# A two-layer decode kernel: filler matmuls in the chain's gaps, the second layer's scores in two halves, a centred x copied out by ScalarE, and the seven-row final FFN placed later

## The chip, the cores and the metric

The kernel runs on one core of a Trainium2 chip. The metric is the device time of one execution in microseconds. A profile records one execution: its span, when each engine was busy, what released each wait, and the clock that TensorE was granted.

## The reference, cut to what matters

Eight sequences (B = 8) each decode one token through two layers that share their weights and caches. A layer is attention over the last 1024 positions of a cache and then an FFN, both with a residual.

```python
x = x + A(layernorm(x))     # wq, softmax over 1024 keys, 16 query heads on 8 kv heads of 256, wo
x = x + B(layernorm(x))     # w1 (448 -> 1792), silu, w2 (1792 -> 448)
x = x + A(layernorm(x))     # the same weights, the same K and V
x = x + B(layernorm(x))

# A, with W = 1024, Dh = 256, D = 448
q = (x @ wq).reshape(B, 1, 16, 256).transpose(0, 2, 1, 3)
k, v = (jnp.repeat(c[:, :, Sk - W:, :], 2, axis=1) for c in (k_cache, v_cache))
p = softmax(einsum("bhqd,bhkd->bhqk", q, k) * 256 ** -0.5)
o = einsum("bhqk,bhkd->bhqd", p, v);  return o.transpose(0, 2, 1, 3).reshape(B, 1, 4096) @ wo
```

A sequence's K and V (8 + 8 tiles of 512 KB) are read once and used by both layers.

## The kernel before, in words

**Loads.** All K and V tiles pass through a ring of R = 30 slots in SBUF. SyncE issues one DMA per tile (K at L467, V at L472) in the order K of sequence b, V of b, K of b+1 and so on. A load waits until the tile that used its slot 30 loads earlier has been read for the last time. K tiles are freed by the second layer's scores of their sequence, V tiles by its second weighted sum. So the 16 loads that follow a sequence's second scores are: the last two V of b+1, the first six K of b+2, and, once its second weighted sum is done too, the last two K and the first six V of b+2.

**One sequence.** VectorE transposes the K tiles in place in blocks (`layer1_early`, L901, 16 instructions). `scores` (L608) multiplies the query blocks `qbd` with K into a PSUM bank: four column tiles of TensorE at once, 8 steps, 32 matmuls of 512 columns for a layer. `softmax` takes the maxima (L613), spreads them by two small transposes, exponentiates on ScalarE (L629), turns the rows into columns by matmuls (L636) and copies them out. `pv_rows` (L658) and `pv_cols` (L685) make the weighted sum of V, `wo_part` (L722) the output projection. For layer 1 the row is then folded onto x (`fold`: ScalarE copies the row at L735, six matmuls of one column at L508 and L511 turn it into columns of bank YB). x sits there as raw columns and, in a sixth column, minus its mean; `xcols` (L696, VectorE) adds the mean, masks the padding and writes the bf16 columns `xbt`.

**The chain.** `feed` and `chain` carry a single token through the first FFN and the query of the second layer, step after step on different engines: `xcols`, `stats` (the variance, off to one side through ScalarE and GpSimd), w1 (L743), copy (L748), turn (`hturn`, L750), tanh (L753), hT (L756, VectorE), w2 (L759), `fold`, `xcols`, wq (L777, 32 matmuls of 512 columns), copy (L783), `q_blocks` (turn at L593, VectorE copy qT2 at L596, selection matmuls at L572, one VectorE product at L598 that writes all of `qbd`), then the second layer's scores, softmax, and weighted sum. While one sequence is in its chain, the next one's layer-1 scores are ready to run, and they are interleaved with the second layer's scores of the first.

**The end.** The second FFN is done for seven sequences at once in `final_rows` (wo of seven rows at L811, w1 at L502, w2 at L835, and so on), whose tasks lie in program order ahead of the last sequence's chain, and for the last sequence alone in `final_last`. Only these two and the last chain have a pair of filler matmuls (`keep`, L729, zero weights, 480 columns).

**Order.** All instructions are tasks of a planner (`Plan`). It knows what each task reads and writes, simulates five in-order queues with the durations in the code, and writes a fixed order for every engine; the most urgent ready task goes first, where urgency is the longest way to the end plus a table of corrections (`BIAS`). On the chip each engine runs its list in that order and waits on semaphores.

Of the kernel before, what the change touches and what calls it, by code (L numbers as in the profile page):

```python
# [4 lines left out]
BF16 = mybir.dt.bfloat16  # L5
# [14 lines left out]
       "dve:max": 0.62, "dve:qbd": 0.62, "act:maskr": 0.13, "act:var4": 0.16, "act:x2b": 0.16, "act:rsum": 0.66,  # L20
# [5 lines left out]
BIAS = {"dve.KT.a": -113.5, "pe.wo.a@7": -369.9, "pe.qsel.b": 390.4, "pe.S0.a": 152.8, "pe.l.c@8": -243.0,  # L26
        "pe.PV0.2.a@7": -51.4, "pe.l.c@7": -192.9, "pe.w18.c": -747.4, "pe.PV1.2.c": 382.0, "dve.hT.b@0": -156.7,
        "dve.qT2.b": -486.8, "dve.oTev.c@1": -161.9, "pe.wq.b": -161.9, "pe.stat.b": 114.3, "pe.stat.b@7": -142.4,
        "pe.PV0.c6.a": 734.8, "pe.PV0.c7.a@0": 159.8, "pe.xres.e": -183.3, "pe.PV1.0.c": -112.1,
        "pe.xinit8.e": -155.3, "pe.fold.a@7": -45.5, "pe.hturn.b": -26.0, "pe.stat.e": 12.5}  # L30
# [237 lines left out]
def bass_interleave_layers__sliding_block_cached__dense_activation_silu__decode_kernel(  # L268
# [9 lines left out]
    P = 128  # L278
# [24 lines left out]
    qbd = [sb(f"qbd{i}", [P, 4, 8, 16], BF16) for i in range(2)]  # L303
# [8 lines left out]
    xb0 = sb("xb0", [P, XC + 1, NB], BF16)  # L312
    f_sb = sb("f_sb", [P, 24], F32)
    b_sb = sb("b_sb", [P, 56], BF16)
# [7 lines left out]
    x2b = xb0  # L322
# [3 lines left out]
    fold8, hT = b_sb[:, 4:12], b_sb[:, 12:28]  # L326
    xl0, nm = b_sb[:, 28:36], b_sb[:, 36:37]
    xz = b_sb[:, 38:53].rearrange("p (c n) -> p c n", n=3)
# [6 lines left out]
    xh = slots[R - 2][:, 512:512 + 2 * XC * NB].rearrange("p (c n) -> p c n", n=2 * NB)  # L335
# [9 lines left out]
    C_Q, C_QT, C_ST, C_HT = 0, 128, 160, 192  # L345
    TW = ((0, 4), (4, 3), (7, 4), (11, 3))
# [46 lines left out]
    dve(lambda e: e.memset(b_sb[:, 38:53], 0.0), [], ["xbt"], 0.08, -98)  # L393
# [90 lines left out]
    def xcol(i, hi):  # L484
        return i if i < 3 else 3 + hi
# [10 lines left out]
    def proj(bank_i, col, outs, lhs, half, rhs, n):  # L496

        fns = []
        for o in outs:
            for i in range(KC):  # L500
                r = rhs(xcol(i, o // half))
                fns.append(lambda e, o=o, i=i, r=r: e.matmul(  # L502
                    bank[bank_i][:, col + (o - outs[0]) * n:col + (o - outs[0] + 1) * n], lhs(o, i), r,
                    start=(i == 0), stop=(i == KC - 1)))
        return fns

    def to_cols(bank_i, col, row, rhs, nb, prio, reads, name, shape):
        fns = [lambda e, c=c: e.matmul(bank[bank_i][xpart(c), col + c * nb:col + (c + 1) * nb], xpiece(row, c), rhs,  # L508
                                       start=False, stop=True, tile_position=xpos(c), skip_group_check=True)
               for c in range(XC)]  # L510
        fns.append(lambda e: e.matmul(bank[bank_i][:, col + XC * nb:col + (XC + 1) * nb],  # L511
                                      row[:, D:D1].broadcast_to([P, P]), rhs, start=False, stop=True,
                                      skip_group_check=True))
        pe(fns, reads, bk(bank_i), shape, prio, name)
# [24 lines left out]

    def start_rows(prio):  # L540
# [4 lines left out]
            for c in range(XC)], ["xrow", "ident"] + L, bk(YB), (NB, 1), prio)  # L545
        m58 = mask5[:].unsqueeze(2).broadcast_to([P, XC, NB])
        dve(lambda e: e.tensor_tensor(xb0[:, 0:XC, :], xp[:, 0:XC * NB].rearrange("p (c b) -> p c b", b=NB), m58,
                                      ALU.mult), bk(YB) + M5, ["xb0"], 0.2, prio)
        stats8(xb0[:, 0:XC, :], sq8, sqh8, vn8, rhalf8, LB, C_ST, NB, ["xb0"] + L, "st", prio, True)
        xcf = big8[:, 0:XC * NB].rearrange("p (c b) -> p c b", b=NB)  # L550
        dve(lambda e: e.tensor_tensor(xcf, xb0[:, 0:XC, :], nmean8.unsqueeze(1).broadcast_to([P, XC, NB]), ALU.add),
            ["xb0", "nmean8"] + L, ["big8"], 0.2, prio)
        dve(lambda e: e.tensor_tensor(xcf, xcf, m58, ALU.mult), ["big8"] + M5 + L, ["big8"], 0.2, prio)
        dve(lambda e: e.tensor_copy(xh[:, :, 0:NB], xcf), ["big8"] + L, ["xh0"], 0.15, prio)
        dve(lambda e: e.tensor_tensor(xh[:, :, NB:], xcf, xh[:, :, 0:NB], ALU.subtract), ["big8", "xh0"] + L, ["xh1"],
            0.2, prio)
        dve(lambda e: e.tensor_copy(xb0[:, XC, :], nmean8), ["nmean8"] + L, ["xm0"], 0.12, prio)
        dve(lambda e: e.tensor_tensor(xl0[:], nmean8, xb0[:, XC, :], ALU.subtract), ["nmean8", "xm0"] + L, ["xl0"], 0.15,
            prio)
        pe(proj(YB, 0, range(NCH), wq_l, 16, lambda i: xh[:, i, :], 2 * NB),  # L560
           ["xh0", "xh1"] + WQ_R + L, bk(YB), (2 * NB, 1), prio, "q1")
# [8 lines left out]
    def q_sel(src, keys, prio):  # L570
        qs = bank[LB][:, C_Q:C_Q + 128].rearrange("p (t a s n) -> p s t a n", t=4, a=2, s=4)
# [4 lines left out]
    def q_view(v):  # L576
        return v.rearrange("p (n r) -> p n r", r=2).unsqueeze(2).broadcast_to([P, 64, 4, 2])

    def q_wide(m):
        return m.unsqueeze(1).unsqueeze(3).broadcast_to([P, 64, 4, 2])  # L580

    qbd_v = [t[:].rearrange("p t c (j q r) -> p (t c j) q r", q=4, r=2) for t in qbd]

    def q_blocks1(b, prio):
        qs = q_sel(q1T[:, b, :].rearrange("p (t n a) -> p t a n", t=4, n=4), [("q1r", b)], prio)
        act(lambda e: e.activation(q1s[:], qs, ACTF.Copy), bk(LB), [("pT", 0)], 0.3, prio, "q1s")  # L586
        add("pool", lambda e: e.tensor_tensor(qbd_v[0], q_view(q1s), q_wide(mask), ALU.mult),  # L587
            reads=[("pT", 0)] + MASK_R, writes=[("qbd", 0)], dur=1.1, prio=prio, name="qbd1")
# [150 lines left out]
    def feed(prio, warm):  # L739
# [14 lines left out]
        if warm:  # L754
            keep(2, prio, XB)
# [222 lines left out]
```

## Time and profile before

| what | value |
|---|---|
| time, three runs | 280.54 us median (278.52 to 284.11) |
| the profiled execution's own time | 282.43 us |
| its span | 280.6 us |
| mean TensorE clock granted | 0.812 |
| TensorE busy | 194.1 us (69%), 2963 matmuls |
| VectorE busy | 152.6 us (54%), of it 82.2 us in the 128 K transposes |
| ScalarE, GpSimd busy | 75.5 us, 21.7 us |
| read from HBM | 77.67 MB, 277 GB/s over the span |

Read it as a pipeline over sequences: a start until the first V tiles are there (48.8 us), then one period for each sequence, then an end in which nothing is loaded any more. The start of the layer-1 maximum (L613) of a sequence marks a period: for sequences 1 to 7 it lies at 72.99, 97.27, 123.68, 151.67, 178.07, 205.18 and 232.89 us. The granted clock is either 1.0 or 0.5 of full speed; the mean of 0.812 mixes the two.

### The profile page before, as it was taken

The numbers are of one execution on the slowest core, as the hardware profiler recorded it, in microseconds if no ns is written. First come the engines' busy times: TensorE is split into PE (matmuls) and PEld (weight loads), VectorE is DVE, ScalarE is ACT, GpSimd is POOL, SyncE is SP. The second block draws the span as 40 slices with busy tenths as digits, with TensorE's granted clock in tenths as the row PEclk, the third lists the DMA queues.
The fourth block names the chain that finished last, engine by engine and source line by source line (L and its number), as shares of the span: only waits on it lengthen the run. The fifth ranks groups of instructions, "written<-read, shape, count | busy, mean of one in ns | idle before, by whom it ended". The sixth has DMA issues, their size and how long they took to land.

```text
span 280.6 us, 6834 instructions
## 1 busy us (share of the span) xinstructions
PE 194.1 (69%) x2963; PEld 84.4 (30%) x2963; DVE 152.6 (54%) x392; ACT 75.5 (27%) x198; POOL 21.7 (8%) x34
## 2 busy tenths in 40 slices
PE   1050400867896887798679868996898588977575
PEld 0050100322442343234223422343234223453231
DVE  6389559249629647733864395538544844122111
ACT  2000729122223133213321331223122313223122
POOL 1200000010011002000200020010001000020000
PEclk9999955755999899669857995797589658999895
DMA  6999999999599979949992999299929993000000
GB/s 254 348 406 357 341 363 388 369 407 387 181 397 370 372 258 409 392 164 310 409 390 92 353 402 386 96 398 403 357 97 369 404 340 120 36 2 3 0 2 0
DMA packets 33757, 78.11 MB, mean 278 GB/s; under 512 B 2224, under 2 KB 8256, under 8 KB 33344
## 3 DMA queue, kind: packets, MB, share of 16 engines
q1 hardware_dynamic: 33728, 77.68, 74.9%
q8 instruction: 23, 0.38, 0.5%
q14 instruction: 6, 0.05, 0.0%
HBM read 77.67 MB, written 0.01 MB: 277 GB/s over the span
## 4 chain that ended last, share of the span: by engine, by line
PE 47%; SPq 15%; DMA 14%; DVE 12%; ACT 8%; issue 3%; POOL 1%; ACTq 0%; DVEq 0%; POOLq 0%
PE bank L608 12%; DMA slot<-in_A_k_cache_dram 10%; PE bank L777 8%; DVE slot L901 8%; PE bank L658 7%; SPq L472 6%; SPq L431 5%; PE bank L722 4%; DMA slot<-in_A_v_cache_dram 4%; PE bank L759 3%; SPq L467 3%; ACT qrow L735 2%; PE bank L685 2%; ACT qrow L783 2%; ACT e_sb L629 2%
## 5 line engine op out<-in xcount | busy, mean ns | idle before, releaser
L901 DVE STREAM_TRANSPOSE slot<-slot 128x512 uint32<-128x512 uint32 x128 | 82.2, 687 | 9.9 <-DMA slot<-in_A_k_cache_dram 9.5
L608 PE MATMUL bank<-slot,qbd 128*16 128x512 bf16 x512 | 43.3, 492 | 8.2 <-DVE slot L901 7.4
L658 PE MATMUL bank<-slot,pT_sb 128*4 128x512 bf16 x448 | 35.8, 408 | 13.9 <-DMA slot<-in_A_v_cache_dram 13.0
L777 PE MATMUL bank<-wq_sb,b_sb 128*2 128x512 bf16 x256 | 27.7, 583 | 0.0
L629 ACT ACTIVATE e_sb<-bank,mseg 128x256 bf16<-128x256 f32 x32 | 13.4, 470 | 46.0 <-DVE mseg L626 25.2
L613 DVE TENSOR_REDUCE mseg<-bank 128x2 f32<-128x512 f32 x16 | 11.1, 691 | 21.9 <-PE bank L608 21.9
L608 PEld LDWEIGHTS bank<-slot,qbd 128*16 128x16 bf16 x512 | 14.0, 102 | 27.8 <-issue 12.8
L587 POOL TENSOR_TENSOR qbd<-pT_sb,f_sb 128x512 bf16<-128x512 bf16 x8 | 8.3, 1041 | 146.2 <-ACT pT_sb L586 146.2
L658 PEld LDWEIGHTS bank<-slot,pT_sb 128*4 128x4 bf16 x448 | 11.1, 87 | 27.5 <-issue 17.9
L759 PE MATMUL bank<-w_sb,b_sb 128*1 128x449 bf16 x126 | 12.0, 473 | 6.5 <-DVE b_sb L756 6.5
L722 PE MATMUL bank<-wo_sb,oT 128*1 128x449 bf16 x256 | 16.2, 360 | 0.0
L707 POOL TENSOR_TENSOR f_sb<-f_sb 128x1 f32<-128x1 f32 x17 | 9.4, 550 | 75.2 <-ACT f_sb L705 75.1
L636 PE MATMUL bank<-ident,e_sb 128*64 128x16 bf16 x256 | 6.8, 179 | 8.2 <-ACT e_sb L629 8.1
L670 DVE TENSOR_TENSOR oT<-bank,rl_sb 128x24 bf16<-128x24 f32 x8 | 1.5, 183 | 20.0 <-PE bank L666 20.0
L586 ACT ACTIVATE pT_sb<-bank 128x128 bf16<-128x128 f32 x8 | 2.2, 278 | 35.1 <-PE bank L685 20.2
L448 DVE TENSOR_REDUCE slot<-wo_sb 128x5 f32<-128x2240 bf16 x4 | 9.7, 2479 | 3.3 <-DMA wo_sb<-in_A_wo_dram 3.3
L508 PE MATMUL bank<-b_sb,qrow 128*128 128x1 bf16 (+1 forms) x85 | 6.2, 181 | 7.6 <-ACT qrow L735 7.6
L689 DVE TENSOR_TENSOR oT<-bank,rl_sb 128x4 bf16<-128x4 f32 x16 | 2.6, 162 | 14.4 <-PE bank L685 14.4
L743 PE MATMUL bank<-w_sb,b_sb 128*1 128x512 bf16 (+1 forms) x144 | 10.1, 375 | 0.3 <-DVE b_sb L696 0.3
L696 DVE SCALAR_TENSOR_TENSOR b_sb<-bank,f_sb 128x5 bf16<-128x5 f32 x17 | 3.8, 224 | 10.9 <-PE bank L511 7.7
L508 PEld LDWEIGHTS bank<-b_sb,qrow 128*128 128x128 bf16 (+1 forms) x85 | 4.5, 106 | 17.2 <-ACT qrow L735 16.9
L783 ACT ACTIVATE qrow<-bank 128x512 bf16<-128x512 f32 x8 | 4.8, 597 | 18.1 <-PE bank L777 18.1
(151 smaller groups left out, 219.1 us busy)
## 6 DMA issues: line engine op xcount, KB each, us to landing
slot<-in_A_k_cache_dram SPq DMA_DIRECT2D x64, 512.0 KB, 9.1
slot<-in_A_v_cache_dram SPq DMA_DIRECT2D x64, 512.0 KB, 9.8
wo_sb<-in_A_wo_dram SPq DMA_DIRECT2D x1, 3584.0 KB, 31.0
wq_sb<-in_A_wq_dram SPq DMA_DIRECT2D x3, 1024.0 KB, 6.9
w_sb<-in_B_w_dram SPq DMA_DIRECT2D x1, 1568.0 KB, 21.2
w_sb<-in_B_w_dram SPq DMA_DIRECT2D x1, 1344.0 KB, 14.2
wq_sb<-in_A_wq_dram SPq DMA_DIRECT2D x2, 256.0 KB, 10.2
w_sb<-in_B_w_dram SPq DMA_DIRECT2D x2, 112.0 KB, 12.8
```

The costliest lines, as they stand in the source:

```text
L431: dma(lambda e: e.dma_start(wo_sb[:].rearrange("p (c n) -> p c n", n=DP)[:, :, 0:D], A_wo.rearrange("(c p) n -> p c n", p=P)), ["wo"], HD ...
L472: dma(lambda e: e.dma_start(slots[s].rearrange("p (q n) -> p q n", q=2), A_v_cache[b, kvh, S0:SK, :].rearrange("(q p uh) d -> p q (uh d)", ...
L508: fns = [lambda e, c=c: e.matmul(bank[bank_i][xpart(c), col + c * nb:col + (c + 1) * nb], xpiece(row, c), rhs, start=False, stop=True, til ...
L608: fns.append(lambda e, c=c, t=t, kv=kv: e.matmul(bank[sc][32 * t:32 * t + 16, :], qbd[layer][:, t, c, :], kv[:, c // 2, c % 2], start=(c = ...
L613: dve(lambda e: e.tensor_reduce(mseg[layer][:, 0:2], bank[sc][:].rearrange("p (k n) -> p k n", k=2), AX.X, ALU.max, negate=True), bk(sc), ...
L629: act(lambda e, k=k: e.activation(e_sb[:, k, :].rearrange("p (uh i ul) -> p uh i ul", uh=4, ul=2), bank[sc][:, k * 256:(k + 1) * 256].rear ...
L658: fns.append(lambda e, c=c, t=t, vv=vv: e.matmul(bank[ob][32 * t:32 * t + 4, :], pT_sb[ei][:, c, t, :], vv[:, c % 2, c // 2], start=(c == ...
L722: fns.append(lambda e, i=i, c=c, kvh=kvh: e.matmul(bank[wb][32 * c:32 * c + 1, 0:D1], oT[:, i % 2, i // 2:i // 2 + 1], wo_sb[:, i * DP:i * ...
L759: pe([lambda e, n=n, t=t, m=m: e.matmul(bank[XB][32 * (n % 4):32 * (n % 4) + 1, 0:D1], hT[:, 4 * m + t:4 * m + t + 1], w2_sb[:, (TW[t][0] ...
L777: pe([lambda e, j=j, c=c, k2=k2: e.matmul(bank[XB][32 * j:32 * j + 2, :], xz[:, xcol(c, k2), 1 - k2:3 - k2], wq_sb[:, c * HD + ((4 * k2 + ...
L783: act(lambda e: e.activation(qrow[:], bank[XB][:], ACTF.Copy), bk(XB), ["rowb"], 0.6, prio, "qrow")
L901: dve(lambda e, v=v: e.transpose(v, v), [("slot", s)], [("slot", s)], 0.67, prio, "KT")
```

## The change

- **Fillers.** `keep` goes; `fill(n)` issues n matmuls of 512 columns with zero weights into bank WB. `feed` has two after w1, three after the turn, two after w2, and `chain` two after wq, for every sequence. A key "row" keeps the chain's matmuls and the fillers in program order among themselves.
- **Scores.** The heads of a column tile are now kvh t and t+4 instead of 2t and 2t+1. Layer 2 computes its scores in two halves of 256 columns (K tiles 0 to 3, then 4 to 7), 64 matmuls instead of 32; layer 1 keeps 32 of 512. `qbd` of layer 2 is written by two VectorE products of half the size, and each half of the steps waits for its own. V is loaded in the order 0, 4, 1, 5, 2, 6, 3, 7. The product that scales the weighted sum (`oTev`) is two instructions instead of one.
- **Centred x.** Bank YB holds x minus its mean, and the mean in column 0. `fold` has eight matmuls instead of six (two more add the mean into the half columns); `xcols` is a plain copy by ScalarE. The copy of minus the mean in `final_last` goes, and qT2 moves from VectorE to ScalarE.
- **Final FFN.** `final_rows` stands behind the last chain and the last scores in program order, and its first matmul waits for the last sequence's second maximum (key "last"). Its VectorE steps for centring become one ScalarE copy.
- **Table.** `BIAS` has other entries, so the planner's order differs in places.

```diff
-    def keep(n, prio, kb):
-        pe([lambda e: e.matmul(bank[kb][:, 16:496], zero_b.broadcast_to([P, P]), wq_sb[:, 0:480],
+    def fill(n, prio):
+        pe([lambda e: e.matmul(bank[WB][:], zero_b.broadcast_to([P, P]), wq_sb[:, 0:512],
                                start=False, stop=True, skip_group_check=True) for _ in range(n)],
-           [("wq", 0), "zero_b"], bk(kb), (480, 1), prio, "keep")
+           [("wq", 0), "zero_b"], bk(WB) + ["row"], (512, 1), prio, "fill")
+    FILL = (2, 3, 2, 2)
...
     # feed: w1
-               ["xbt"] + W1_R, bk(XB), (448, 4), prio, "w1")
+               ["xbt"] + W1_R, bk(XB) + ["row"], (448, 4), prio, "w1")
         act(lambda e: e.activation(qrow[:], bank[XB][:], ACTF.Copy), bk(XB), ["rowb"], 0.6, prio, "w1row")
+        fill(FILL[0], prio)
...
         act(lambda e: e.activation(th, ht, ACTF.Tanh, scale=rhalf), bk(LB) + ["rhalf"], OT1, 0.31, prio, "tanh")
-        if warm:
-            keep(2, prio, XB)
+        fill(FILL[1], prio)
...
     # feed: behind w2
+        fill(FILL[2], prio)
...
     # chain: behind wq
         act(lambda e: e.activation(qrow[:], bank[XB][:], ACTF.Copy), bk(XB), ["rowb"], 0.6, prio, "qrow")
+        fill(FILL[3], prio)
         q_blocks(prio)
...
     def xcols(prio):
-        dve(lambda e: e.scalar_tensor_tensor(out=xbt, in0=bank[YB][:, 0:XC], scalar=bank[YB][:, XC:XC + 1],
-                                             in1=mask5[:], op0=ALU.add, op1=ALU.mult), bk(YB) + M5, ["xbt"], 0.23, prio,
-            "xb")
+        act(lambda e: e.activation(xbt, bank[YB][:, 0:XC + 1], ACTF.Copy), bk(YB), ["xbt"], 0.25, prio, "xb")
...
     def q_blocks(prio):
-        dve(lambda e: e.tensor_copy(qT2, bank[LB][:, C_QT:C_QT + 32]), bk(LB), OT1, 0.18, prio, "qT2")
+        act(lambda e: e.activation(qT2, bank[LB][:, C_QT:C_QT + 32], ACTF.Copy), bk(LB), OT1, 0.25, prio, "qT2")
...
-        dve(lambda e: e.tensor_tensor(qbd_v[1], q_view(qs), q_wide(maskr), ALU.mult), bk(LB) + ["maskr"], [("qbd", 1)], 0.7, prio,
-            "qbd")
+        for a in range(2):
+            dve(lambda e, a=a: e.tensor_tensor(qbd_v[1][:, 32 * a:32 * a + 32], *q_wide(qs[:, 64 * a:64 * a + 64], maskr),
+                                               ALU.mult), bk(LB) + ["maskr"], [("qbd", 1, a)], 0.4, prio, "qbd")
...
     def scores(b, layer, prio):
         sc = SC[layer]
-        for c in range(8):
+        for ks in ((slice(0, 2),) if layer == 0 else (slice(0, 1), slice(1, 2))):
+            for c in range(8):
...
+                    kv = kslots[:, s + 4 * ks.start:s + 4 * ks.stop - 3:4, c // 2, c % 2]
+                    fns.append(lambda e, c=c, t=t, kv=kv, ks=ks: e.matmul(
+                        bank[sc][32 * t:32 * t + 16, 256 * ks.start:256 * ks.stop], qbd[layer][:, c, t, :], kv,
+                        start=(c == 0), stop=(c == 7), tile_position=(0, 32 * t)))
...
     # to_cols, used by fold
+        fns += [lambda e, c=c: e.matmul(
+            bank[bank_i][xpart(c), col + (c + 1) * nb:col + (c + 2) * nb], m.broadcast_to([P, 64]), rhs,
+            start=False, stop=True, tile_position=xpos(c), skip_group_check=True) for c in (3, 4)]
...
     for b in range(NB):
         if b < NB - 1:
             layer1_early(b + 1)
-        else:
+        chain(b, 100 * b + 60)
+        if b == NB - 1:
+            scores(b, 1, 100 * b + 60.5)
             orow7 = final_rows(NB - 1, 100 * b + 90)
-        chain(b, 100 * b + 60)
         layer2(b)
```

## The prediction, made before the changed kernel was run

> **What bounds the kernel now.** I read first the page's slices, then a table of windows, then TensorE's timeline for one sequence, then SyncE's waits. In the slices, TensorE is busy almost throughout and its clock swings between 9 and 5; the DMA engines have a hole in each period from the sixth on.
>
> ```profile
> PE   1050400867896887798679868996898588977575
> PEclk9999955755999899669857995797589658999895
> DMA  6999999999599979949992999299929993000000
> ```
>
> The windows below are 3.41 us wide, because the openings of the clock that I found in half-microsecond windows (52.4, 69.5, 93.2, 124.1, 151.4, 178.7, 206.0, 233.3) lie on one grid of that step. Columns: length, then TensorE busy, weight loads, VectorE, ScalarE, GpSimd; granted clock, DMA share, GB/s.
>
> ```profile
> 185.54:188.95 3.41, 3.41 (x78) 1.66 (x74) 1.64 (x5) 0.43 (x2) 1.04 (x1) 1.00 1.03 414
> 188.95:192.37 3.42, 2.41 (x42) 1.27 (x34) 3.04 (x8) 1.74 (x4) 0.55 (x1) 1.00 1.02 408
> 192.37:195.78 3.41, 2.03 (x21) 0.70 (x20) 3.07 (x6) 0.91 (x2) 0.00 (x0) 0.50 1.01 400
> 195.78:199.19 3.41, 3.08 (x33) 0.99 (x35) 3.22 (x6) 0.75 (x3) 0.55 (x1) 0.50 1.05 386
> 199.19:202.61 3.42, 2.71 (x32) 0.73 (x28) 0.30 (x2) 0.60 (x1) 0.00 (x0) 0.50 1.05 385
> 202.61:206.02 3.41, 3.41 (x36) 1.11 (x32) 1.38 (x3) 0.00 (x0) 0.00 (x0) 0.50 0.16 59
> ```
>
> A window with 2.41 us busy closes the gate to half speed; then 3.08 busy is not enough to open it, a full 3.41 is. So the closing falls into the chain, whose gaps make TensorE idle, and wq and the scores pay for it. The timeline shows where (start, length, instruction, idle before it):
>
> ```profile
> 192.12 0.26 PE L750 MATMUL bank<-ident,qrow 128*128 128x4 bf16 x4 [0.71 <-ACT qrow L748]
> 193.02 1.66 PE L759 MATMUL bank<-w_sb,b_sb 128*1 128x449 bf16 x14 [0.65 <-DVE b_sb L756]
> 195.42 0.39 PE L508 MATMUL bank<-b_sb,qrow 128*128 128x1 bf16 x5 [0.73 <-ACT qrow L735]
> 196.46 1.03 PE L777 MATMUL bank<-wq_sb,b_sb 128*2 128x512 bf16 x8
> 197.56 2.73 PE L777 MATMUL bank<-wq_sb,b_sb 128*2 128x512 bf16 x24
> 201.00 0.28 PE L593 MATMUL bank<-ident,qrow 128*128 128x8 bf16 x4 [0.71 <-ACT qrow L783]
> ...
> 254.77 1.90 PE L777 MATMUL bank<-wq_sb,b_sb 128*2 128x512 bf16 x32
> ```
>
> The same 32 wq matmuls take 3.83 us here (196.46 to 200.29) and 1.90 in the last sequence, where the gate stayed open. DMA is second: SyncE's waits are for TensorE, not the reverse.
>
> ```profile
> SPq L472 <- PE bank L572: 70.0, 6, 12.8
> SPq L467 <- PE bank L658: 31.0, 6, 6.0
> ```
>
> Sixteen loads of 0.524 MB at the 395 GB/s of the busy windows need 21.2 us; a period takes (232.89 - 72.99)/6 = 26.65. The pace of the loads is the floor under this change.
>
> **The fillers.** The four gaps before L750, L759, L508 and L593 idle 0.71, 0.65, 0.73, 0.71 us. A full-speed matmul of 512 columns takes 0.215 (w1: 16 in four columns, 1.03 with a tail of 0.17, so 0.215 for a group). Two fill 0.43, three 0.64: at open gate all fit, price zero. The cover is the copies and the tanh; at half clock a filler takes 0.43, two need 0.86 and three 1.28, so the cover is short by 0.15, 0.63, 0.13 and 0.15. The filler queues the turn, w2, the fold or the query turn behind it on TensorE, and all of these are on the chain. With 0.43 more, the window at 188.95 comes to 2.84 of 3.42. Windows of 2.53 to 2.66 at 243.56, 250.39, 72.90 and 151.41 stayed open, one of 2.19 (257.22) too, and one of 2.43 (52.42) closed: I take it that the gate stays open.
>
> Per period that gives: wq 3.83 to 1.90, saving 1.93; the layer-1 scores, from their first matmul to the maximum, 3.98 (119.70 to 123.68) to 2.39 as in the second sequence (94.88 to 97.27), saving 1.59; w2 1.66 to 0.93 where it was slow, saving 0.73. Chains 3, 5 and 6 have all three, 4.25 each; chains 2 and 4 ran w2 at full speed, 3.52 each; chain 1 found the gate open again before its scores and saves only 3.39 - 1.90 = 1.5 in wq. Sum 12.75 + 7.05 + 1.5 = **21.3 us**.
>
> [...]
>
> **Start.** Chain 0 begins at half clock, so fillers cost there until a window is full. They make 59.25:62.66 (2.05 busy) almost full; the gate would open then instead of at 69.5, saving up to 2.6 on w2 and wq against about 0.8 of fillers. But the next scores (70.6) come right behind nine K transposes in one run (65.11 to 70.56), and VectorE stood before them for 1.58 us on the tanh. Between 0 and 2 us: I take **1.0**.
>
> **Scores in halves.** No row has 256 columns in four tiles. Above, a step costs no more than one of 512, 0.215, so 16 steps 3.4 us against 1.7; below, half, 1.7. The nearest row is L636 (16 pairs in 0.42) with L685 (16 pairs with full weights in 0.56): 0.027 us a pair, 0.108 for four, equal to half a step. I take zero. It is covered as well: the layer-1 softmax needs 2.5 us from its last score to its first matmul (178.07 to 180.55), the other layer's scores fill 1.7 of them; at the upper bound 0.9 a period shows, 5 in all. Loads keep count and tiles; V tiles 3 and 7 remain the last two, and SyncE still issues them first after the scores, with their consumer L685 4.8 us later as before.
>
> [...]
>
> **Centred x.** Two more matmuls in each fold, 0.045 apiece by L508 (five in 0.35 with the tail): +0.18 a period. `xcols` goes from 0.224 on VectorE to 0.197 on ScalarE (the row of L770, also 128x6), and no longer stands behind a transpose of 0.69: the start lay 0.04 to 0.47 after L511's end, about 0.1 on average. Behind the copy on ScalarE stand only the x2b copy and the variance, which need it anyway. qT2 on ScalarE 0.25 against 0.186; the halved product lets step one start 0.35 earlier. One more oTev, 0.18, lies beside L685. Bounds -0.5 to +0.3 a period; I take zero.
>
> **What is late next.** With the chain 3.5 shorter, the K tiles come into view. In the fifth sequence VectorE waited for a K tile until 170.81 and ended its transposes at 172.7; the scores started at 174.09 and would now start at 172.16. That is 0.55 late there, nothing in the third (transposes end 117.83). I add 0.3 for each of six periods: **+1.8**; the upper bound, 0.7 each, is 4.2.
>
> **The end**, from 232.89: the seven-row wo (1.69 at 242.84) leaves the way of the last layer-1 output. From the maximum to the row copy 245.34 - 232.89 = 12.45 becomes 188.80 - 178.07 = 10.73: -1.7. The last chain loses the other final matmuls: row copy to first second-layer score 13.64 becomes 4.22 (188.80 to 193.02) + 5.32 (7.98 to the query turn less 0.73 and 1.93) + 1.25 = 10.8: -2.85. The moved wo now fills the 2.54 us gap before 263.55, so the gate need not close at 264.3 and the weighted sum drops from 3.43 to 1.9: -1.5. The copy of the mean goes: -0.3. The last w2 at full speed and its fillers: -0.9. Against it, 5.9 us of moved matmuls must find room in some 6 us of gaps; +1.0, at most +3. Sum **-6.25**. The new wait "last" holds only these seven rows, whose output is issued ahead of the last row's on SyncE; by their chain of some 11 us after the maximum they are done about 5 us before it.
>
> **Sum**, against the profiled execution's own 282.43 (span 280.6 and 1.8 around it): 282.43 - 21.3 - 1.0 + 1.8 - 6.25 = 255.7. The median of the runs shown lies 1.9 lower than that execution, which gives **254 us**.
>
> **Rivals.**
> *The loads set the pace.* If the rest shrinks more than I think, six periods of 21.2 are 127.2 instead of 140.4, hence 241. For it: hardly a hole is left in the DMA row. Against: the next scores come only 22 to 23 us after the last.
> *The gate closes in about half of the chains.* Then half of 21.3 and the 1.5 of the weighted sum go: 266. For it: the folds, stats and turns count as busy but carry one to eight columns, and 2.43 closed once.
> *The gate stays shut in the chain as now.* Place: the three fillers before w2 and the two before the fold and the query turn, at half clock, 0.63 + 0.13 + 0.15 = 0.9 for each of eight chains, +7.3; the end then gains nothing, as the last chain turns slow too (+4.3 against -2.85 and the rest): about 289, slower than before. It decides from the point where fewer than 0.9 of 4.8, a fifth of the chains, stay open. For it: fillers with zero weights stood at 274.5 and ran at half clock. Against: their window had followed one with 2.06 busy, and the last chain, with fillers and other work, stayed open for four windows.
>
> **How the numbers follow.** Forecast 0.57, loads 0.12, half open 0.20, shut 0.06; 0.05 is left for things between that end within 2%. The range goes from 244, the forecast with part of the loads' case, to 270, half open with the upper bounds on late K and the end. A measurement of this kernel can tell about 2% from no change; faster by more than that 0.89, within 0.05, slower 0.06.
>
> **What would show it.** In the changed profile the clock should read 1.0 through the middle, wq 1.9 and w2 0.93 for each sequence, maxima 22 to 24 us apart, and DMA holes of 1 to 2 us. It is wrong if wq still takes 3.8, if the second scores take over 2.2 at full clock, or if TensorE waits for K or V by more than 1 us a period.

## The result, and the profile after

The changed kernel takes 265.13 us at the median of four runs (260.68 to 266.52), the kernel before 282.33 beside it: ratio 0.940, 95% interval 0.922 to 0.959, so 6% faster. Further runs of the same kernel in two other sittings gave 263.02 and 262.35 us (ratios 0.929 and 0.925). Medians are over all runs; ratios use only the fast ones, those within 1.5% of the fastest run of the same kernel. The profiled execution took 260.68 us, its span is 258.9, and the mean granted clock rose from 0.812 to 0.941.

The slices first. TensorE is busy from the tenth slice on, its clock is 9 almost throughout behind the start, and the DMA row, which had a hole to 4 or 2 around each of the third to sixth layer-1 maxima (119 to 210 us), now falls to 5 at the lowest before the last load.

```profile
PE   1050340478887898998699989789997996998686
PEclk9999985555999999999799999999999999999999
DMA  6999999999969995999978999999999999000000
```

One chain in TensorE's timeline (start, length, instruction, idle before it):

```profile
169.78 2.10 PE L618 MATMUL bank<-slot,qbd 128*16 128x256 bf16 x64
173.51 1.90 PE L671 MATMUL bank<-slot,pT_sb 128*4 128x512 bf16 x24 [0.30 <-DMA slot<-in_A_v_cache_dram]
...
182.67 0.60 PE L740 MATMUL bank<-wq_sb,b_sb 128*128 128x512 bf16 x2
183.56 0.81 PE L740 MATMUL bank<-wq_sb,b_sb 128*128 128x512 bf16 x3
184.34 0.93 PE L770 MATMUL bank<-w_sb,qrow 128*1 128x449 bf16 x14
187.06 1.90 PE L788 MATMUL bank<-wq_sb,b_sb 128*2 128x512 bf16 x32
```

L740 are the fillers; they fill the gaps before the turn, w2, the fold (but for 0.20 us) and the query turn. The 14 matmuls of w2 take 0.93 us and the 32 of wq 1.90, the times they had at full clock before (87.79 and 254.77 us). The first line is the second layer's scores in halves: 64 matmuls in 2.10 us, where 32 of twice the columns took 2.03 at full clock before. The second line has something new: the first weighted sum waits for a V tile.

That wait comes back in five of six periods. TensorE's and SyncE's waits between 73 and 216 us (total, times, longest):

```profile
PE bank L671 <- DMA slot<-in_A_v_cache_dram: 3.3, 5, 1.9
```

```profile
SPq L472 <- PE bank L618: 55.9, 7, 10.1
SPq L467 <- PE bank L715: 33.7, 5, 9.0
```

SyncE still waits longest for TensorE: 55.9 us on the issue of V, where it was 70.0 before, and 33.7 on the issue of K, where it was 26.5 in this stretch. So the loads wait for their slots much as before, and now TensorE waits for the loads too.

All profiles can be compared by three numbers: the start of the first layer-1 maximum, the six periods to the seventh, and the rest to the end of the span (all in us).

| kernel | first maximum | six periods | to the end | mean clock |
|---|---|---|---|---|
| before | 72.99 | 159.9 | 47.7 | 0.812 |
| changed | 72.86 | 142.0 | 44.1 | 0.941 |
| changed, e1_again | 71.72 | 143.9 | 45.3 | 0.941 |
| changed, e9_after_again | 71.42 | 144.9 | 44.8 | 0.961 |
| e2_b_fill | 73.41 | 140.3 | 51.4 | 0.956 |
| e3_nofill | 72.80 | 155.2 | 45.1 | 0.864 |
| e4_half_v | 70.74 | 145.1 | 44.3 | 0.941 |
| e5_half_v_same_order | 70.50 | 137.0 | 44.2 | 0.953 |
| e6_s1_whole | 73.00 | 184.2 | 53.1 | 0.846 |
| e7_wo8_last | 70.40 | 142.1 | 44.5 | 0.993 |
| e8_slow_plan | 74.74 | 145.7 | 45.7 | 0.929 |
| e10_s1_whole_same_order | 72.59 | 144.4 | 44.6 | 0.987 |
| e11_final_first | 72.31 | 140.8 | 53.9 | 0.974 |
| e12_one_filler | 70.29 | 151.6 | 43.6 | 0.936 |

The last column can't be compared over all rows. In e2, e6, e7, e9, e10 and e11 no clock is recorded for the start, and the profile then counts full speed. The same stretch from 44 to 53 us shows it, first in e7_wo8_last and then in the changed kernel's first profile: the 24 matmuls take 3.58 us in both, as at half clock, beside a granted clock of 1.00 and 0.50 (columns as in the prediction).

```profile
44.00:53.00 9.00, 3.58 (x24) 0.95 (x24) 6.71 (x7) 5.56 (x20) 0.00 (x0) 1.00 1.05 399
44.00:53.00 9.00, 3.58 (x24) 0.93 (x24) 6.82 (x7) 5.57 (x20) 0.00 (x0) 0.50 1.04 399
```

The means of these six rows are too high by some 0.03 to 0.05 (an estimate: half speed from about 36 us to the first record, at 53 to 64 us). The periods, from about 73 us on, are not touched by it.

### The profile page after: what moved, and what is told of

Its sections match the earlier page's. It is cut to its first block, busy times and chain, and to the rows that moved or that the text cites. A ratio compares the mean times of both kernels' runs of the same rounds, so it can differ in the third digit from the quotient of the medians.

```text
span 258.9 us, 7574 instructions
## 1 busy us (share of the span) xinstructions
PE 189.8 (73%) x3330; PEld 93.6 (36%) x3330; DVE 149.6 (58%) x388; ACT 79.1 (31%) x223; POOL 21.6 (8%) x34
## 4 chain that ended last, share of the span: by engine, by line
PE 36%; DMA 32%; SPq 24%; ACT 4%; issue 2%; DVE 2%
DMA slot<-in_A_v_cache_dram 29%; SPq L472 13%; PE bank L671 12%; PE bank L733 6%; SPq L431 5%; SPq L467 4%; DMA slot<-in_A_k_cache_dram 3%; PE bank L699 3%; PE bank L618 2%; PE bank L740 2%; ACT qrow L676 2%; PE bank L754 1%; PE bank L788 1%; PE bank L508 1%; PE bank L770 1%
## 5 line engine op out<-in xcount | busy, mean ns | idle before, releaser
L618 PE MATMUL bank<-slot,qbd 128*16 128x256 bf16 (+1 forms) x768 | 34.7, 323 | 2.8 <-DVE q1T L686 1.5
L740 PE MATMUL bank<-wq_sb,b_sb 128*128 128x512 bf16 x79 | 24.0, 396 | 0.0
L618 PEld LDWEIGHTS bank<-slot,qbd 128*16 128x16 bf16 x768 | 18.4, 89 | 10.8 <-issue 2.2
L671 PEld LDWEIGHTS bank<-slot,pT_sb 128*4 128x4 bf16 x448 | 10.8, 86 | 28.4 <-issue 20.2
L686 DVE TENSOR_TENSOR oT<-bank,rl_sb 128x12 bf16<-128x12 f32 x16 | 2.7, 171 | 25.1 <-PE bank L679 24.8
L592 ACT ACTIVATE pT_sb<-bank 128x128 bf16<-128x128 f32 x8 | 2.2, 278 | 46.3 <-PE bank L579 24.4
L788 PE MATMUL bank<-wq_sb,b_sb 128*2 128x512 bf16 x256 | 15.2, 378 | 0.0
L605 DVE TENSOR_TENSOR qbd<-bank,f_sb 128x256 bf16<-128x256 f32 x16 | 6.1, 420 | 14.4 <-PE bank L579 14.4
L648 PE MATMUL bank<-ident,e_sb 128*64 128x16 bf16 x256 | 6.8, 179 | 6.2 <-ACT e_sb L641 6.2
L648 PEld LDWEIGHTS bank<-ident,e_sb 128*64 128x64 bf16 x256 | 5.3, 112 | 12.6 <-ACT e_sb L641 9.2
L699 PE MATMUL bank<-pT_sb,slot 128*128 128x2 bf16 x256 | 8.9, 164 | 1.3 <-DVE oT L704 1.3
L740 PEld LDWEIGHTS bank<-wq_sb,b_sb 128*128 128x128 bf16 x79 | 5.0, 98 | 12.6 <-issue 11.6
```

The lines of the kernel that those rows point to most:

```text
L618: fns.append(lambda e, c=c, t=t, kv=kv, ks=ks: e.matmul(bank[sc][32 * t:32 * t + 16, 256 * ks.start:256 * ks.stop], qbd[layer][:, c, t, :] ...
L648: pe([lambda e, k=k, uh=uh, h=h: e.matmul(pt[64 * h:64 * h + 64, k, uh], e_sb[:, k, uh * 64:uh * 64 + 64], rows[:, k, h], start=True, stop ...
L671: fns.append(lambda e, c=c, t=t, vv=vv: e.matmul(bank[ob][32 * t:32 * t + 4, :], pT_sb[ei][:, c, t, :], vv[:, c % 2, c // 2], start=(c == ...
L699: fns.append(lambda e, a=a, c=c, o=o: e.matmul(bank[sc][:, c0 + 2 * a:c0 + 2 * a + 2], vs[:, o:o + P], pT_sb[ei][:, c, t, 2 * k:2 * k + 2] ...
L740: pe([lambda e: e.matmul(bank[WB][:], zero_b.broadcast_to([P, P]), wq_sb[:, 0:512], start=False, stop=True, skip_group_check=True) for _ i ...
L788: pe([lambda e, j=j, c=c, k2=k2: e.matmul(bank[XB][32 * j:32 * j + 2, :], xz[:, xcol(c, k2), 1 - k2:3 - k2], wq_sb[:, c * HD + ((4 * k2 + ...
```

## The experiments

### How much is the clock: fillers alone, all but the fillers

`e1_again` and, in a later sitting, `e9_after_again` are the changed kernel itself, as yardsticks.

> The changed kernel once more, unchanged, as the base for what runs beside it. Both theories: 0.93 to 0.95 of before, 262 to 267 us. If the profiled execution is a slower one than the 260.7 us profiled first, its trace should show where the scatter lies: theory V (the V loads set the pace) expects the same clock near 0.95 and longer waits of L671 for V; the rival expects a lower clock with gates that close.

> The changed kernel as it is, a second time, as the yardstick for the three kernels beside it. Both theories: 263 us at the median, 258 to 267, ratio 0.93 to 0.94; from the last layer-1 maximum to the end 44 to 45 us; periods of 23 to 24 us.

Measured: 263.02 us (256.48 to 267.25) and 262.35 (261.06 to 264.68). Both things that e1_again was to tell apart were seen in its profile: TensorE waited 4.2 us for V in the periods (3.3 in the first profile), and the gate closed (the granted clock fell from 1.00 to 0.50) twice between 66 and 240 us instead of once.

`e2_b_fill` is the kernel before with nothing but the fillers, and these only in the chains of the first seven sequences; behind w1, the turn, w2 and wq; the keys that hold them in their places come with them.

```diff
+    FILL = (2, 3, 2, 2)
+    def fill(i, prio):
+        if prio < 100 * (NB - 1):
+            pe([lambda e: e.matmul(bank[WB][:], zero_b.broadcast_to([P, P]), wq_sb[:, 0:512],
+                                   start=False, stop=True, skip_group_check=True) for _ in range(FILL[i])],
+               [("wq", 0), "zero_b"], bk(WB) + ["row"], (512, 1), prio, "fill")
...
+        fill(0, prio)
...
+        fill(1, prio)
...
+        fill(2, prio)
...
+        fill(3, prio)
```

> The kernel before with nothing but the fillers (two, three, two, two) in the chains of sequences 0 to 6; the last chain keeps its old pair. Theory clock (the fillers hold the gate open, and that is nearly the whole gain of the periods): wq 1.9 us in all chains, periods near 23.7, end unchanged at 47 to 48 us after the last layer-1 maximum, 265 to 269 us. Rival (the fillers alone do little, the gain comes from the halves, ScalarE and the new order): 276 to 283 us, wq still 3.8 in most chains.

`e3_nofill` is the changed kernel without any filler: `FILL = (0, 0, 0, 0)`.

> The changed kernel without any filler. Theory clock: the gate closes in the chains, wq 3.8 us again, periods 26 to 27, 276 to 284 us. Rival (the other parts carry the gain): 263 to 269 us.

Measured: e2_b_fill 266.65 us (261.99 to 268.67), ratio 0.947 [0.929, 0.965]; e3_nofill 279.92 (274.77 to 283.89), ratio 0.999 [0.990, 1.008]. The clock row of the page, first of the old kernel with fillers (its first eight slices are the start, for which no clock is recorded):

```profile
PEclk9999999999889999999999999999999998959795
```

and of the changed kernel without them:

```profile
PEclk9999985685999999869986995998599959999568
```

Together with before and after this makes a table of two by two. By the medians of one sitting, fillers bring the old kernel from 281.12 to 266.65 us and the new one from 279.92 to 263.02; all the rest of the change brings 1.2 without fillers and 3.6 with them. By the profiles, fillers bring the six periods from 159.9 to 140.3 us in the old kernel and from 155.2 to between 142.0 and 144.9 in the new one, and the rest brings nothing there once fillers are in. (155.2 is low for that kernel: the profiled execution of e3_nofill, 274.77 us, was the fastest of twelve.) The 32 matmuls of wq tell how: 1.90 us in all eight chains of the changed kernel's first profile (one of 3.17 in e9_after_again), 3.27 to 3.58 in six of the eight of e3_nofill. In e2_b_fill they come in two pieces of together some 2.1 us in the first seven chains. One chain of e3_nofill, then one of e2_b_fill:

```profile
195.29 3.58 PE L789 MATMUL bank<-wq_sb,b_sb 128*2 128x512 bf16 x32
```

```profile
115.06 0.60 PE L788 MATMUL bank<-wq_sb,b_sb 128*2 128x512 bf16 x8
115.73 1.47 PE L788 MATMUL bank<-wq_sb,b_sb 128*2 128x512 bf16 x24
```

So the fillers are the gain in the periods, and the clock is how they make it. In the last chain of e2_b_fill, where the old pairs stand alone, the clock row falls to 5; its end takes 51.4 us, not the 47 to 48 that were expected, and that is what keeps it behind the changed kernel.

`e12_one_filler` gives each gap one filler, 0.86 us in a chain instead of 1.93: `FILL = (1, 1, 1, 1)`.

> One filler in each of the four gaps instead of 2, 3, 2, 2, so 4 and not 9 in a chain, 0.86 us of work instead of 1.93. Theory that a window of 3.41 us closes the gate at about 2.4 us busy: the chain's emptiest windows rise to some 2.8 to 3.1, the gate stays open in most chains, 262 to 268 us. Rival, that the gaps themselves must be filled (no gap above some 0.4 us): the gate closes in most chains as without fillers, 272 to 280 us.

Measured: 270.47 us (267.24 to 272.03), ratio 0.949 [0.942, 0.956], between the two cases and above what the first theory gave. The gate closed in four windows behind 66 us, at 88.8, 112.7, 215.1 and 249.2. The three periods with a closing are 25.5, 26.9 and 26.3 us, those without 24.0, 24.6 and 24.4. The second group is still longer than the 22.8 us of an undisturbed period of the changed kernel (mean of its three without a closing in e9_after_again), and TensorE's waits show another reason:

```profile
PE bank L770 <- DVE qrow L767: 6.4, 6, 1.6
```

w2 now waits in every period for hT (L767), which stands on VectorE behind a run of K transposes; around 160 us these had themselves waited 0.97 and 0.56 us for their tiles. e3_nofill has the same wait, 5.1 us in five. The planner writes a new order when durations change, so neither kernel is a pure price of the clock: up to 5 or 6 us of the loss are order.

### What sets the period now: the V tiles

`e4_half_v` loads only half of each V tile from the third sequence on, by a transfer of half the size.

```diff
+    FULL_V = {(b, k) for b in range(2) for k in range(8)}
...
+        if (b, kvh) not in FULL_V:
+            dma(lambda e: e.dma_start(slots[s][:, 0:1024],
+                                      A_v_cache[b, kvh, S0:S0 + W // 2, :].rearrange("(p uh) d -> p (uh d)", uh=4)),
+                [("slot", s)], W * DH, "slot%d" % s, rate=387e3)
+            return
```

> The changed kernel with V loaded only by half (positions 0 to 511) for sequences 2 to 7; the other half of a V slot keeps old data. So 8 loads of a period carry half the bytes; all else is as it was. Theory V (V tiles that arrive late set the period): L671's waits for V vanish, periods fall from 23.7 to 22.3 to 22.8, minus 5 to 9 us against the changed kernel, 256 to 260 us. Rival (TensorE and the chain set the period, the waits only show slack): within 2 us of the changed kernel.

Measured: 265.16 us (261.92 to 271.38), ratio 0.951 [0.939, 0.964]: no gain, which seems to clear the loads. It does not. TensorE waits 0.3 us for V in these periods, but the planner was told of half the bytes too, and put the transposes of K earlier into VectorE's queue. There they wait for K and hold up the chain:

```profile
DVE slot L913 <- DMA slot<-in_A_k_cache_dram: 9.7, 14, 1.7
```

(4.1 us in the changed kernel.) `e5_half_v_same_order` moves the same bytes and tells the planner the full number, `W * DH * 2`, so that the order stays.

> As the half-V run (V of sequences 2 to 7 loaded only for positions 0 to 511, the other half of the slot keeps old data), but the planner still reckons with whole V tiles, so every engine's order is that of the changed kernel and only the bytes differ. Theory V (late V tiles cost the periods what the forecast missed there): L671's waits for V between 73 and 216 us fall from 3.3 to 4.2 us to under 0.5, no gate closes behind them, periods 22.2 to 22.8, 4 to 8 us under the changed kernel. Rival (the chain on TensorE sets the pace even so): periods stay at 23.3 to 23.7 and the time within 2 us.

Measured: 257.01 us (253.43 to 260.23), ratio 0.907 [0.901, 0.914]. The six periods fall to 137.0 us; but for the first, in which the gate closed once, they are 22.3 to 22.9. The waits over the same stretch of 73 to 216 us:

```profile
PE bank L677 <- DMA slot<-in_A_v_cache_dram: 0.8, 1, 0.8
```

So the late loads cost the changed kernel 5 to 8 us. It is V in the first place; but with half of V's bytes K comes earlier too, and VectorE's wait for K falls as well, which this run does not separate. Over the same stretch, in the changed kernel and here:

```profile
DVE slot L907 <- DMA slot<-in_A_k_cache_dram: 4.1, 5, 1.3
DVE slot L913 <- DMA slot<-in_A_k_cache_dram: 1.4, 3, 0.6
```

The late V tiles come in a loop: the first six V of a sequence can only be issued when the second weighted sum two sequences earlier has freed their slots (SyncE's wait at L467 above). In the changed kernel these sums end at 109.4, 135.6, 158.0 and 181.6 us, 24 us apart in the mean: from one of them the issue of two K and six V takes about 4.5 us, the slowest of their transfers 9.9 to 11.4, and the chain from the first weighted sum behind them to the next second one some 8.5. As long as a period took 26.65 us this loop was hidden.

Some late tiles are paid for twice. In e9_after_again the weighted sum behind two waits runs at half clock:

```profile
148.31 3.57 PE L671 MATMUL bank<-slot,pT_sb 128*4 128x512 bf16 x24 [1.85 <-DMA slot<-in_A_v_cache_dram]
196.01 3.52 PE L671 MATMUL bank<-slot,pT_sb 128*4 128x512 bf16 x24 [0.89 <-DMA slot<-in_A_v_cache_dram]
```

3.57 instead of 1.90, so the wait of 1.85 costs 3.5. In the three profiles of the changed kernel the gate closed six times between 66 and 240 us; five of the six were at such a wait, the sixth behind a wait of w2 for hT (1.45 us at 88.32 in e9_after_again), which stood behind K transposes that had waited for K.

`e8_slow_plan` tells the planner slower loads, 380 and 370 instead of 411.2 and 387 GB/s, so that it would expect the late tiles.

```diff
-    def dma(fn, writes, n_bytes, key, reads=(), rate=411.2e3):
+    def dma(fn, writes, n_bytes, key, reads=(), rate=380e3):
...
-                [("slot", s)], W * DH * 2, "slot%d" % s, rate=387e3)
+                [("slot", s)], W * DH * 2, "slot%d" % s, rate=370e3)
```

> The changed kernel with the planner told that K and V loads run at 380 and 370 GB/s instead of 411 and 387, so that it orders the work for tiles that come later; in every second period the second layer's weighted sum then stands beside the first's. Theory (in-order queues stall on tiles that land later than the plan has them): 2 to 6 us under the changed kernel. Rival (the loads set the pace whatever the order): within 2 us, with the waits moved from one engine to another.

Measured: 265.6 us (263.21 to 267.86), ratio 0.939 [0.933, 0.945]. The wait for V shrinks to 1.0 us, and the time is not better: other waits take its place (5.4 us before L648 for the exponentials, which were 2.1). The theory's 2 to 6 us did not come: here the planner that knew of the lateness moved it and did not remove it.

### Do the halves of the scores cost or bring anything

`e6_s1_whole` puts the second layer's scores back into one piece and drops the correction that went with their first half.

```diff
-        for ks in ((slice(0, 2),) if layer == 0 else (slice(0, 1), slice(1, 2))):
+        for ks in (slice(0, 2),):
...
-BIAS = {"pe.S1.0.b": -1489.7, "dve.KT.a@1": 301.0, "pe.stat.b": 733.7, "pe.PV0.c3.a@0": -568.3, "pe.PV1.1.c": -52.1,
+BIAS = {"dve.KT.a@1": 301.0, "pe.stat.b": 733.7, "pe.PV0.c3.a@0": -568.3, "pe.PV1.1.c": -52.1,
```

> The changed kernel with the second layer's scores in one piece again (32 matmuls of 512 columns; the products that write qbd stay halved; the table's entry for the first half is dropped). Theory clock (halves cost and bring nothing): within 1% of the changed kernel, the scores from first matmul to maximum 1.9 to 2.1 us as in halves. Rival (halves bring a part of the gain): 3 us or more above the changed kernel, periods above 24.

Measured: 310.59 us (305.44 to 312.11), ratio 1.090 [1.079, 1.101]. That is no price of the halves. Without the correction the second layer's scores are urgent, and in every second sequence the next one's layer-1 scores move into the gaps of the chain, where they need K too early (over the whole run):

```profile
DVE slot L907 <- DMA slot<-in_A_k_cache_dram: 24.1, 12, 5.0
```

The periods alternate between 29 and 32 us. `e10_s1_whole_same_order` keeps the correction, and with it, but for some groups of four or eight matmuls, TensorE's order (VectorE's and ScalarE's still differ in places); only the first line of the diff is left.

> The second layer's scores in one piece of 32 matmuls of 512 columns, the late place in the queue kept, so that TensorE's order stays that of the changed kernel. Theory that the halves cost nothing: the piece takes 1.9 to 2.1 us instead of 2.1, the first maxima stay 23 to 24 us apart, the time is that of the yardstick within 2 us. Rival, the halves cost: each of the 16 steps has up to 0.1 us more than half a step, so the one piece saves 0.4 to 0.9 a period and the kernel comes 3 to 6 us under the yardstick. Second rival, the halves pay: the first half frees four of eight K tiles about 1 us earlier, so the loads start earlier; then the one piece makes the periods 0.5 to 1 us longer and the kernel comes 3 to 6 us above the yardstick.

Measured: 262.68 us (258.85 to 264.15), ratio 0.917 [0.910, 0.924], beside the yardstick's 262.35 and 0.925 [0.920, 0.931]. The intervals overlap. The ratios differ by 0.008, some 2.4 us in favour of the one piece, and their intervals leave room for anything from about nothing to some 5 us. So that the halves pay by 3 us is excluded; that they cost 3 is not excluded by the times. In the timeline the whole piece takes

```profile
169.05 2.02 PE L618 MATMUL bank<-slot,qbd 128*16 128x512 bf16 x32
```

against 2.10 in halves, and the second maximum starts 2.15 us after the first instead of 2.20: 0.05 a period, 0.3 in six. The trace thus speaks for a price near nothing. Freeing four K tiles earlier brought nothing that can be seen.

### The end

In the last chain of the changed kernel stand four pieces of the seven-row wo (L822), in front of the scores:

```profile
230.35 0.56 PE L822 MATMUL bank<-wo_sb,q1T 128*7 128x449 bf16 x8
...
232.14 0.56 PE L822 MATMUL bank<-wo_sb,q1T 128*7 128x449 bf16 x8
...
233.15 0.56 PE L822 MATMUL bank<-wo_sb,q1T 128*7 128x449 bf16 x8
...
236.23 0.56 PE L822 MATMUL bank<-wo_sb,q1T 128*7 128x449 bf16 x8
...
238.06 2.06 PE L618 MATMUL bank<-slot,qbd 128*16 128x256 bf16 x64 [0.52 <-DVE qbd L605]
```

`e7_wo8_last` makes them wait for the last maximum as well.

```diff
-               [(("q1r", b), h) for b in range(nb) for h in range(2 * k2, 2 * k2 + 2)] + WO_R, bk(SC[0])
+               ["last"] + [(("q1r", b), h) for b in range(nb) for h in range(2 * k2, 2 * k2 + 2)] + WO_R, bk(SC[0])
```

> The changed kernel with the seven-row wo also waiting for the last sequence's second maximum, as the forecast had taken it to do. Theory (the four pieces of it inside the last chain are what that chain takes longer): from the row copy to the first second-layer score 12.2 becomes about 11.2 us, and the gap before the softmax's matmuls is filled; the end 0 to 1.5 us shorter, the whole time within 1%. Rival (the pieces sit in gaps): that stretch stays at 12.2 and the end grows by 1 to 2 us.

Measured: 260.89 us (258.61 to 264.18), ratio 0.922 [0.915, 0.929]. From the start of the fold (L508) to the first score, the last chain takes 10.57 us, in the changed kernel 11.54, in the kernel before 12.68. The wo is now one piece behind the maximum:

```profile
235.26 2.06 PE L618 MATMUL bank<-slot,qbd 128*16 128x256 bf16 x64 [0.52 <-DVE qbd L605]
238.12 0.20 PE L819 MATMUL bank<-xh,ident 128*128 128x42 bf16 x1 [0.80 <-DVE mseg L624]
238.25 1.70 PE L822 MATMUL bank<-wo_sb,q1T 128*7 128x449 bf16 x32
```

and from the first score to the end it is 21.74 instead of 20.84. What the chain wins, 0.97, the last stretch loses, 0.90: the end is 44.5 us, as it was. The median, 1.5 to 4.2 us under those of the other sittings, is within the scatter.

`e11_final_first` puts the seven-row FFN back in front of the last chain, with the fillers kept (in another bank there).

```diff
+        else:
+            orow7 = final_rows(NB - 1, 100 * b + 90)
         chain(b, 100 * b + 60)
         if b == NB - 1:
             scores(b, 1, 100 * b + 60.5)
-            orow7 = final_rows(NB - 1, 100 * b + 90)
```

> The FFN of the first seven rows put back in front of the last chain, without the wait for the last maximum; the last chain's fillers use another bank. Theory (the prediction's end term, as corrected): the stretch from the last layer-1 maximum to the end grows from 44.1 to 46 to 48 us, the periods stay, so the kernel comes 2 to 4 us above the yardstick. By the prediction's own terms (1.7 and 2.85 less 1.0) it would be 3.5, the weighted sum's 1.5 not counted. Rival, the move gains nothing, since the loads of the last V tiles set the stretch: end 43 to 45, yardstick within 1.5 us.

Measured: 268.49 us (265.11 to 274.75), ratio 0.942 [0.936, 0.948], 6.1 above the yardstick beside it, more than expected. The periods stay (140.8), the end grows to 53.9. From the fold to the first score are 19.1 us, and the reason stands in the timeline:

```profile
235.81 1.66 PE L843 MATMUL bank<-w_sb,slot 128*7 128x448 bf16 x14 [1.03 <-DVE slot L841]
236.90 2.08 PE L771 MATMUL bank<-w_sb,qrow 128*1 128x449 bf16 x14
```

The seven rows' own steps wait on VectorE (1.09 and 1.03 us) in front of the last sequence's w2, the stretch from 231.0 to 234.4 has 2.05 us busy, and the gate is shut from about 234 to 241. Most of the 7.6 us over the changed kernel is the rows' place: from the end of w1 to the start of w2 are 7.7 us, in the changed kernel 2.0, and 5 of the 7.7 pass before the gate closes. The half clock adds some 2 behind it (9.2 instead of 7.3 us from w2 to the first score). In the kernel before, the planner had the rows' w2 behind that of the last sequence, the gate stayed open, and the stretch was 12.68. So this run prices its own order and not the move alone; what the move is worth, between 1 us (12.68 to 11.54) and nearly 8 in that stretch, stays open.

## Why the prediction was right and where it was not

**The number.** 254 us was forecast, 244 to 270 given as the range, and 265.13 came. That is inside, but of the 26.5 us that the forecast took off the median only 17.2 came, two thirds. The mechanism was right; the end, the late tiles and the step to the median were off, as follows.

**The clock, right.** The step said that the gate stays open with fillers, wq takes 1.9 and w2 0.93, and six periods fall from 159.9 to 140.4. They take 142.0 in the profile, 143.9 and 144.9 in the two repeats. e2_b_fill, with the fillers alone, gives 140.3. e3_nofill, with all but the fillers, gives 155.2.

**What is late next, the wrong tile and the wrong size.** The term took +1.8 for late K and left V as it was, looking only at V's last two tiles. Late are the first six, which wait for the second weighted sum to free their slots. In the profiled execution the six periods lose 3.3 us to that wait and 1.6 to the half clock behind it (3.54 instead of 1.90 once); by e5_half_v_same_order all late loads together cost 5 to 8. That the six periods came out within 1.6 us of the sum all the same is in part luck, two errors that cancel: with V on time the periods are 22.5 us and not the 23.1 that the prediction had before its late loads, nor the 23.4 of the fillers alone. So something in the rest of the change, taken at zero, seems to shorten the chain by up to 0.9 a period, and the late tiles take it back. Part of the 0.9 may be waits for loads in e2_b_fill, which moves whole tiles (0.6 us for V and 1.8 for K in its six periods). Which part of the change it is, the copies on ScalarE or the halved product, was not separated; that it is one of these is only argued.

**Halves and fillers at zero, right as far as the traces show.** The halves cost 0.05 us a period in the trace of e10_s1_whole_same_order. The fillers fit: from the end of w1 to the turn are 0.71 us with two of them (110.53 to 111.24), as before without (191.41 to 192.12). The 64 matmuls of the halves take 2.10 us, 33 ns each.

**The start.** -1.0 was taken; the first maximum lies at 72.86, 71.72 and 71.42 in the three profiles instead of 72.99, so -0.1 to -1.6.

**The end, the step that failed.** -6.25 was taken, -3.65 came (47.7 to 44.1), 2.6 short. In parts: maximum to row copy 10.95 for 10.73, with 1.23 us of waiting for V in it. Row copy to first score 12.3 for 10.8: the prediction let "the moved wo" fill the gap behind the last maximum and so took all of the seven rows' matmuls out of the chain, but the new wait is on the first of them alone (L819), and wo does not hang on it: its four pieces stayed in the chain. First score to the end 20.84 for 19.9: the weighted sum was to drop by 1.5, and the stretch from it to the turn before wo drops by 0.6 (3.5 us for 4.1), as the seven rows' w1 of 1.58 us stands in it. e7_wo8_last shows that the middle part could be had only at the price of the last: 0.97 us won there, 0.90 lost behind it. The seven-row wo cost about 1 us in both places.

**The profiled execution and the median.** The sum for the profiled execution was 255.7; it took 260.7, and the periods, the start and the end account for the 5.0 (1.6, 0.9 and 2.6 short, rounded). The other 6 lie in the last line: the prediction put the median 1.9 us under the profiled execution, as before, and it came 4.45 above it. That step had only the scatter of single executions behind it: the execution profiled after the change was the fastest of its four. Seventeen executions of the changed kernel have spans of 254.7 to 265.5 us, and their mean clock goes with it loosely (correlation -0.68; where the start's clock is not recorded the mean is too high, as said above). One closing more or less makes 2 to 3 us (25.5 against 22.8 for a period of e9_after_again), which fits that scatter, though it was not shown run by run.

**The rivals.** "The gate closes in half of the chains" gave 266, next to what was measured, and is not what happened: in the profile with 142.0 it closes once, and not in a chain; of all six closings in the three profiles one came in a chain. "The loads set the pace" was right about who is next, though not at the bytes' pace of 21.2 us a period: it is the round of slot, issue and landing that takes longer.

## What to carry to other kernels

Gaps of 0.7 us on TensorE, in which the chain only waited for another engine, cost some 3.3 us a period here by the clock (159.9 to 140.3 in six periods), so count busy time in windows of 3.41 us, the step that the openings showed here, and fill the emptiest ones, before anything else in the chain is shortened. When a chain shrinks by an eighth, follow each buffer through its whole round (last read, issue, landing, first read) for all tiles and not only the last, since here a round that was hidden came to set the period (142.0 us for six, 137.0 with half of V's bytes). And where a planner writes the order, changing a duration or one correction changes the order: hold it fixed, or the experiment prices something else (8 us hidden in e4_half_v, 265.16 against 257.01; 48 us made up in e6_s1_whole, 310.59 against 262.68).

## What the runs showed of the hardware

**One wait, with and without a fall of the clock.** In the changed kernel the granted clock falls to 0.50 at 126.00 and is back at 1.00 from 129.41. Windows of 3.41 us, the step of the prediction, on a grid through these two times (length, busy time of TensorE, weight loads, VectorE, ScalarE, GpSimd; clock, DMA share, GB/s):

```profile
119.18:122.59 3.41, 3.41 (x92) 2.14 (x84) 2.04 (x7) 0.46 (x2) 0.00 (x0) 1.00 0.98 372
122.59:126.00 3.41, 0.82 (x24) 0.55 (x23) 1.82 (x7) 1.50 (x5) 0.00 (x0) 1.00 1.01 353
126.00:129.41 3.41, 3.41 (x26) 0.90 (x22) 0.00 (x0) 0.00 (x0) 0.00 (x0) 0.50 1.00 389
```

Softmax gaps and a wait of 1.86 us for V fall into one window, 0.82 busy, and the next runs at half clock. In e7_wo8_last the same wait, also 1.86 us, at 145 to 147 us, falls on both sides of a border of the grid laid over that profile (2.24 and 2.01 busy), and the clock stays at 1.00. The two waits and, under them, the two windows of e7_wo8_last:

```profile
125.91 3.54 PE L671 MATMUL bank<-slot,pT_sb 128*4 128x512 bf16 x24 [1.86 <-DMA slot<-in_A_v_cache_dram]
146.91 1.90 PE L671 MATMUL bank<-slot,pT_sb 128*4 128x512 bf16 x24 [1.86 <-DMA slot<-in_A_v_cache_dram]
```

```profile
142.10:145.51 3.41, 2.24 (x73) 1.58 (x61) 2.47 (x12) 1.35 (x4) 0.00 (x0) 1.00 0.96 339
145.51:148.92 3.41, 2.01 (x35) 0.86 (x36) 0.19 (x1) 0.67 (x3) 0.00 (x0) 1.00 1.05 401
```

**Busy time in a window and the clock in the next.** I laid a grid of this step over six profiles (before, changed, e3_nofill, e7_wo8_last, e9_after_again, e12_one_filler) and took every window at full clock from about 50 us on (in e7_wo8_last and e9_after_again from their first clock record). Of those under 1.5 us busy, 10 of 10 were followed by half clock; from 1.5 to 2.0, 8 of 12; from 2.0 to 2.5, 9 of 52, the fullest with 2.47; above 2.5, none of 228. Of the windows at half clock, none under 2.6 was followed by full clock, and all above 3.3 were. So in these windows busy time, as the profile counts it, goes with the clock at both ends and doesn't settle it in between; no run shows what decides there.
